# Sinkhorn-sorted attention with a StarReLU layer behind it: the first microseconds reordered, the last outputs cut finer

## The chip, the cores and the metric

The kernel runs on one core of one Trainium2 chip. A core has five engines that run their own instruction queues in order: TensorE (matrix products, with weight loads listed as PEld), VectorE (DVE), ScalarE (ACT), GpSimd (POOL) and SyncE (SP). TensorE writes to PSUM; VectorE and ScalarE copy from PSUM to SBUF. DMAs are issued from SyncE's and GpSimd's queues. The metric is the device time of one execution in microseconds (us). Three runs of the kernel before took 223.43, 222.94 and 223.51 us; the median is 223.43.

## The reference

Four batches, eight heads, 768 tokens, head size 64. Each head has an 8 by 8 sorting matrix, made nearly doubly stochastic by five rounds of Sinkhorn; it mixes blocks of 96 keys and of 96 values, and each block of queries attends to its sorted block alone. The outputs of all heads side by side go through a layer of width 2048.

```python
P = sort_net
for _ in range(5):
    P = P - np.max(P, axis=-1, keepdims=True)
    P = np.exp(P)
    P = P / (np.sum(P, axis=-1, keepdims=True) + 1e-09)
    P = P / (np.sum(P, axis=-2, keepdims=True) + 1e-09)
k_sorted = np.einsum('bhij,bhjcd->bhicd', P, k_b)      # v_sorted likewise
scores = scale * np.matmul(q_b, k_sb.transpose(0, 1, 2, 4, 3))
attn = softmax(scores)                                  # per block, + 1e-09 in the sum
x = np.matmul(attn, v_sb)                               # heads side by side: 3072 x 512
r = np.maximum(x @ w_in, 0.0)
out = (s * (r * r) + b) @ w_out                         # 3072 x 512, float32
```

## The kernel before, in words

The order of the work is written out by hand: each engine runs its instructions in the order in which the program issues them, and buffers come from rotating pools. In PSUM, pool `psa` has three tiles of two banks (keys, values, scores, `pv`, hidden sums) and pool `psb` two tiles of one bank (transposes, half key pieces, scores in banks, outputs). A tile of a pool can be written only when the tile that last had its buffer has been read.

**Loads.** SyncE loads the sorting matrices (L77) and the values of batch 0 in four quarters of 12 columns, `v0f` (L81). GpSimd issues all other loads: half of the queries (`qh`), the keys in three parts (`rawk`), then, after small constants, `w_in` in slices (`wi`, L142), the other half of the queries, `w_out`, and data of batch 1. GpSimd's issues hold on for older loads: at most eight are under way.

**Front, batch 0, first half.** TensorE begins with matmuls on zeros (`warm`, L132): 16 of 256 columns, 108 of 96, 6 of 512. Meanwhile VectorE and ScalarE run Sinkhorn on `sn`, 32 heads on 32 partitions (L231 to L253); between its exponentials ScalarE casts the quarters of `v0f` into `VP[0]` (`permute`, L196). Then `spread_first` copies batch 0's rows to 128 partitions by a matmul (`pe`, L259), and `build_pd` (L275 to L284) makes of them a block-diagonal matrix `pd` with which a matmul sorts, divided by a sum `cs` for the rounding left by the last, unfinished column step.

After that come, in this order: query transposes `q_banks` (L218); key tiles of 16 columns, two of a full `psa` tile (`k_piece`, L294) and one in two banks (`k_banks`, L320); the first of four value tiles (`v_piece`, L330); the rows of all four batches spread into a corner of a score tile and copied to `later` (`spread_all`, L259 and L271); scores of the first two head pairs (`s_banks` L399, `s_piece` L381) with their exponentials; the other value tiles; scores of the other pairs; per head pair the product with the values, divided by its sum (`p_piece`, L423 to L429), and its transpose to `xt` (`t_piece`, L440); and the first two double columns of the hidden layer, by head pairs (`part`, L474). `evac` copies a PSUM tile with the engine named by its letter, "D" for VectorE (L206) and "A" for ScalarE (L204). A number after the head pair in `p_piece` and `part` asks for so many fill matmuls on zeros before the real ones (L417, L469).

**Dense part.** Then come, for each half batch t of 384 tokens, `ffn1` (hidden layer, ReLU on ScalarE, square on VectorE) and `ffn2` (second product, `ops`, L498), with the attention work of the following halves put in slots between them. For batches 2 and 3 the values are sorted as rows, and `v_back` sends them through a DRAM buffer `vd` (L355) to the layout `VS` (L359); the query transposes by DMA (L457) stand behind it in SyncE's queue.

**End.** The last half batch has three row groups of 128 tokens. The last of them is computed in two halves of 256 output columns (L511). `store` scales by `s` and adds the bias on VectorE (L519) and issues the DMA (L522).

## Time and profile before

| What | Value |
|---|---|
| profiled execution | 223.59 us |
| its span | 221.8 us |
| median of three runs | 223.43 us (222.94 to 223.51) |
| TensorE busy | 214.8 us, 97% of the span |
| VectorE, ScalarE, GpSimd busy | 123.3, 106.1, 70.6 us |
| first `tqb` transposes of the dense part start | 26.43 us |
| last matmul of the program starts | 218.13 us |
| last DMA is issued, lands | 218.95, 220.66 us |

The profile is of one execution. Times are counted from the span's start. In rows of the timeline the columns are start, duration (of a merged run of like instructions: from the first start to the last end), engine, line, operation, output and inputs, shapes, the number of instructions, and in brackets how long the engine was idle before and what ended that. In rows of the chain they are start, length, engine and line. In rows by line, what stands behind the bar is busy time, mean length of one instruction in ns, and idle time before. Matmuls are pipelined: one starts before the one ahead has ended, so the distance of their starts tells the occupancy, not their length.

### The profile page before, as it was taken

The numbers are of one execution on the slowest core, as the hardware profiler recorded it, in microseconds if no ns is written. First come the engines' busy times: TensorE is split into PE (matmuls) and PEld (weight loads), VectorE is DVE, ScalarE is ACT, GpSimd is POOL, SyncE is SP. The second block draws the span as 40 slices with busy tenths as digits, with TensorE's granted clock in tenths as the row PEclk, the third lists the DMA queues.
The fourth block names the chain that finished last, engine by engine and source line by source line (L and its number), as shares of the span: only waits on it lengthen the run. The fifth ranks groups of instructions, "written<-read, shape, count | busy, mean of one in ns | idle before, by whom it ended". The sixth has DMA issues, their size and how long they took to land.

```text
span 221.8 us, 5257 instructions
## 1 busy us (share of the span) xinstructions
PE 214.8 (97%) x2212; PEld 129.6 (58%) x2231; DVE 123.3 (56%) x251; ACT 106.1 (48%) x144; POOL 70.6 (32%) x127
## 2 busy tenths in 40 slices
PE   7999999999999999999999999999999999999993
PEld 5977766555655555666446555655446556654453
DVE  6767457549754767546616677548417744442121
ACT  4677687656144344664622535665424355650000
POOL 7659791669914004930032008800000000000000
PEclk9999999999999999999999999999999999999999
DMA  6999999999999632999999546999911440001212
GB/s 154 280 165 126 125 162 207 204 177 117 116 182 165 183 96 46 138 236 127 91 252 171 138 121 91 236 147 92 221 69 50 121 120 0 0 3 47 95 47 95
DMA packets 66935, 28.92 MB, mean 130 GB/s; under 512 B 51808, under 2 KB 62816, under 8 KB 66912
## 3 DMA queue, kind: packets, MB, share of 16 engines
q0 software_dynamic: 31168, 12.85, 49.6%
q1 hardware_dynamic: 35744, 15.74, 34.3%
q8 instruction: 17, 0.28, 0.6%
q14 instruction: 6, 0.05, 0.1%
HBM read 28.85 MB, written 7.86 MB: 165 GB/s over the span
## 4 chain that ended last, share of the span: by engine, by line
PE 95%; DVE 2%; issue 1%; ACT 0%
PE hps L474 38%; PE ops L498 36%; PE z L132 5%; PE pv L423 4%; PE sc L381 3%; PE ops L511 2%; PE tv L330 2%; PE tp L294 1%; PE tpp L304 1%; PE tvr L349 1%; DVE vs L206 1%; PE tr L440 1%; PE scb L399 1%; PE sc L259 0%; PE pv L417 0%
## 5 line engine op out<-in xcount | busy, mean ns | idle before, releaser
L474 PE MATMUL hps<-xt,wi 128*128 128x384 bf16 x512 | 87.9, 326 | 0.0
L498 PE MATMUL ops<-wo,gt 128*128 128x512 bf16 x350 | 82.4, 379 | 1.5 <-issue 0.8
L486 ACT ACTIVATE rt<-hps 128x768 bf16<-128x768 f32 x64 | 51.8, 811 | 39.5 <-PE hps L474 38.8
L474 PEld LDWEIGHTS <-wi 128*128 128x128 bf16 x512 | 49.0, 98 | 32.6 <-issue 0.4
L487 DVE TENSOR_TENSOR gt<-rt 128x768 bf16<-128x768 bf16 x64 | 35.6, 558 | 41.2 <-ACT rt L486 41.0
L498 PEld LDWEIGHTS <-gt 128*128 128x128 bf16 x368 | 34.0, 98 | 37.2
L519 DVE SCALAR_TENSOR_TENSOR ot<-ops,s_bc,bias 128x512 f32<-128x512 f32 (+1 forms) x25 | 18.2, 729 | 37.9 <-PE ops L498 34.4
L389 ACT ACTIVATE at<-sc 112x768 bf16<-112x768 f32 x24 | 18.1, 808 | 31.8 <-PE sc L381 31.8
L429 DVE TENSOR_TENSOR x<-pv,rec 96x512 bf16<-96x512 f32 x32 | 22.0, 687 | 1.1
L116 POOL DMA_DIRECT2D qtok<-in_q_dram x24 | 18.6, 810 | 0.7 <-DMA rawk<-in_k_dram 0.6
L423 PEld LDWEIGHTS <-at 112*128 112x128 bf16 (+1 forms) x256 | 12.9, 101 | 6.7 <-ACT at L389 1.0
L142 POOL DMA_DIRECT2D wi<-in_moe_w_in_dram x24 | 13.0, 583 | 6.0 <-DMA qh<-in_q_dram 3.1
L423 PE MATMUL pv<-vs,at 112*128 112x66 bf16 (+1 forms) x256 | 13.9, 195 | 0.1
L93 POOL DMA_DIRECT2D rawk<-in_k_dram x21 | 11.2, 551 | 4.3 <-DMA rawv<-in_v_dram 2.0
L132 PE MATMUL z<-zeros 128*64 128x96 bf16 (+2 forms) x129 | 10.8, 257 | 1.3 <-DVE zeros L120 1.2
L93 POOL DMA_DIRECT2D rawv<-in_v_dram x18 | 9.7, 555 | 5.5 <-DMA wo<-in_moe_w_out_dram 4.7
L204 ACT CAST ks<-tpp 64x512 bf16<-64x512 f32 x12 | 8.7, 725 | 4.4 <-DVE ks L206 4.1
L132 PEld LDWEIGHTS <-zeros 128*64 128x64 bf16 (+1 forms) x130 | 8.5, 128 | 3.0 <-DVE zeros L120 1.2
L90 POOL COPY rawk<-xt 128x1 bf16<-128x1 bf16 x2 | 0.4, 190 | 31.1 <-DMA xt<-x 31.1
L428 DVE RECIPROCAL rec<-pv 96x8 f32<-96x8 f32 x32 | 6.4, 200 | 6.4 <-PE pv L423 6.4
L206 DVE CAST ks<-tpp 64x512 bf16<-64x512 f32 x12 | 8.7, 728 | 0.2
L351 DVE CAST rawv<-tvr 128x512 bf16<-128x512 f32 x12 | 8.2, 683 | 0.0
(93 smaller groups left out, 141.6 us busy)
## 6 DMA issues: line engine op xcount, KB each, us to landing
out_dram<-ot SPq DMA_DIRECT2D x23, 256.0 KB, 2.5
rawv<-in_v_dram POOLq DMA_DIRECT2D x18, 128.0 KB, 5.1
rawk<-in_k_dram POOLq DMA_DIRECT2D x18, 128.0 KB, 4.5
qtok<-in_q_dram POOLq DMA_DIRECT2D x24, 96.0 KB, 6.7
wo<-in_moe_w_out_dram POOLq DMA_DIRECT2D x4, 512.0 KB, 10.4
v0f<-in_v_dram SPq DMA_DIRECT2D x4, 384.0 KB, 7.1
vd<-rawv SPq DMA_DIRECT2D x2, 768.0 KB, 6.8
vs<-vd SPq DMA_DIRECT2D x8, 192.0 KB, 7.4
```

The source lines that it names most:

```text
L93: nc.gpsimd.dma_start(out=ti[:, c:c + n, :].rearrange("p c d -> p (c d)"), in_=raw["qkv".index(t)][b][:, c * D:(c + n) * D])
L116: nc.gpsimd.dma_start(out=ti[:, n + h], in_=qv[:, n + h])
L132: nc.tensor.matmul(out=z[0:m, 0:w], lhsT=zeros[:, 0:m], rhs=zeros[:, 0:w], start=True, stop=True)
L142: nc.gpsimd.dma_start(out=wi[:, al, f0:f1], in_=wiv[:, al, f0:f1])
L389: nc.scalar.activation(out=at, in_=sc[0:KR, :, 0:TG], func=AF.Exp, scale=scale)
L423: nc.tensor.matmul(out=pv[0:m, e, n * VW:(n + 1) * VW], lhsT=atf[:, c0:c0 + m], rhs=VS[b % 2][:, e * NG + g0 + n, :], start=True, stop=True)
L429: nc.vector.tensor_tensor(out=x[:, :, hp * 128:(hp + 1) * 128].rearrange("p n (e d) -> p e n d", e=2), in0=pvv[:, :, :, 0:D], in1=rec.unsq ...
L474: nc.tensor.matmul(out=H1[t, i][:, f, 0:TG], lhsT=wi[:, hp, fc:fc + 128], rhs=XT[t][:, :, hp, :], start=(hp == 0), stop=(hp == NHP - 1))
L486: nc.scalar.activation(out=rt, in_=h, func=AF.Relu)
L487: nc.vector.tensor_tensor(out=gt[:, 2 * i:2 * i + 2, :], in0=rt, in1=rt, op=ALU.mult)
L498: nc.tensor.matmul(out=ops, lhsT=gt[:, f, m * 128:(m + 1) * 128], rhs=wo[:, f, :], start=(f == 0), stop=(f == NF - 1))
L519: nc.vector.scalar_tensor_tensor(out=ot[:, ns], in0=ops, scalar=s_bc, in1=BIAS[0][:, ns], op0=ALU.mult, op1=ALU.add)
```

## The change

In the front: 1e-9 stands as a ninth row in the Sinkhorn tile, so the first column sum takes it in and the separate add goes. `build_pd` gets its sum `cs` from the product itself (`accum_out`) in place of a second reduce. The warm-up has 132 matmuls of 72 columns in place of 108 of 96. The third quarter of `v0f` is cast by GpSimd, behind four `wi` issues. The first value tile is issued ahead of the key tiles, and ScalarE empties it; the spread of the three later batches gets a tile of its own between key tiles and half key pieces; value tiles 3 and 4 are emptied half by ScalarE and half by VectorE; scores 2 and 3 use whole tiles and stand between the p pieces; fill matmuls are gone; `part` takes two head pairs at once. `v_back` sends the two halves of the partitions as two DMAs and reads them back in that order. At the end, the last but one row group is stored in two halves, and the last row group is computed and stored in 256, 128 and 128 columns.

```diff
-    sn = const.tile([BH, NB, NB], FP)
+    sne = const.tile([BH, NB + 1, NB], FP)
+    sn = sne[:, 0:NB, :]
...
     for c in range(4):
         for a in range(NHP):
             load_wi(c * W8, (c + 1) * W8, slice(a, a + 1))
+        if c == 0:
+            permute(nc.gpsimd, 0, v0f, slice(2 * CV, 3 * CV))
...
-    eps = const.tile([BH, NB], FP)
-    nc.vector.memset(eps, 1e-9)
+    nc.vector.memset(sne[:, NB:NB + 1, :], 1e-9)
...
-    warm(108, 96, 64)
+    warm(132, 72, 64)
...
-        for c in {1: (0,), 3: (1,), 4: (2, 3)}.get(it, ()):
+        for c in {1: (0,), 3: (1,), 4: (3,)}.get(it, ()):
...
-        nc.vector.tensor_reduce(out=rstat, in_=sn.rearrange("p i j -> p j i"),
+        nc.vector.tensor_reduce(out=rstat, in_=(sn if it else sne).rearrange("p i j -> p j i"),
                                 axis=AX.X, op=ALU.add)
-        if it == 0:
-            nc.vector.tensor_tensor(out=rstat, in0=rstat, in1=eps, op=ALU.add)
...
-    def spread_all(ps):
-        for b in range(B):
-            o = TG + b // 2 * NB * NB
-            spread_rows(b, ps[:, b % 2, o:o + NB * NB])
-        nc.scalar.copy(out=later.rearrange("p u w n -> p u (w n)"), in_=ps[:, :, TG:512])
+    def spread_later():
+        pe = psa.tile([128, B - 1, NB * NB], FP, tag="a", name="pel")
+        for b in range(1, B):
+            spread_rows(b, pe[:, b - 1, :])
+        return lambda: nc.scalar.copy(out=later, in_=pe)
...
-        nc.vector.tensor_tensor(out=tmp, in0=rows.rearrange("p (i j) -> p i j", j=NB),
-                                in1=spread(jsel, [[0, NB], list(jsel.ap[1])]), op=ALU.mult)
+        cs = rtp.tile([128, 1], FP, tag="cs", name="cs")
+        nc.vector.scalar_tensor_tensor(
+            out=tmp, in0=rows.rearrange("p (i j) -> p i j", j=NB), scalar=1.0,
+            in1=spread(jsel, [[0, NB], list(jsel.ap[1])]), op0=ALU.mult, op1=ALU.mult, accum_out=cs)
         pt = rtp.tile([128, NB], FP, tag="pt", name="pt")
         nc.vector.tensor_reduce(out=pt, in_=tmp, axis=AX.X, op=ALU.add)
-        cs = rtp.tile([128, 1], FP, tag="cs", name="cs")
-        nc.vector.tensor_reduce(out=cs, in_=pt, axis=AX.X, op=ALU.add)
...
-        nc.sync.dma_start(out=vd.rearrange("e z g c d -> (e z g) (c d)"),
-                          in_=RAW["v", b].rearrange("p c d -> p (c d)"))
-        for z in range(2):
-            for e in range(2):
+        for e in range(2):
+            nc.sync.dma_start(out=vd[e].rearrange("z g c d -> (z g) (c d)"),
+                              in_=RAW["v", b][e * 64:(e + 1) * 64].rearrange("p c d -> p (c d)"))
+        for e in range(2):
+            for z in range(2):
...
-                    if f == NF - 1:
+                    if f == NF - 1 and last and m == TG // 128 - 2:
+                        for n0 in range(0, d_model, d_model // 2):
+                            ns = slice(n0, n0 + d_model // 2)
+                            store(t, m, ops[:, ns], ns)
+                    elif f == NF - 1:
                         store(t, m, ops)
...
-            for n0 in range(0, d_model, d_model // 2):
-                ns = slice(n0, n0 + d_model // 2)
-                ops = psb.tile([128, d_model // 2], FP, tag="b", name="ops")
+            for n0, w in ((0, 256), (256, 128), (384, 128)):
+                ns = slice(n0, n0 + w)
+                ops = psb.tile([128, w], FP, tag="b", name="ops")
...
     q_banks(0, 0, "DA")
+    v_piece(0, 0, "A")
     k_piece(0, 0, "D")
     k_piece(0, CK, "A")
+    copy_later = spread_later()
     k_banks(0, 2 * CK, "DA")
-    v_piece(0, 0, "D")
-    sc1 = psa.tile([128, 2, 512], FP, tag="a", name="sc")
-    spread_all(sc1)
+    copy_later()
     s_banks(0, 0, 0)
-    s_piece(0, 0, 1, sc1)
+    s_piece(0, 0, 1)
     v_piece(0, CK, "D")
-    v2 = v_piece(0, 2 * CK, "D", 1)
+    v2 = v_piece(0, 2 * CK, "A", 1)
+    v2("D")
     v3 = v_piece(0, 3 * CK, "A", 1)
-    v2("D")
-    s_banks(0, 0, 2)
-    p_piece(0, 0, 0, 3)
-    v3("A")
-    p_piece(0, 0, 1, 2)
-    s_banks(0, 0, 3)
-    p_piece(0, 0, 2, 2)
+    v3("D")
+    s_piece(0, 0, 2)
+    p_piece(0, 0, 0)
+    s_piece(0, 0, 3)
+    p_piece(0, 0, 1)
+    p_piece(0, 0, 2)
     t_piece(0, 0, 0, "A")
-    p_piece(0, 0, 3, 3)
+    p_piece(0, 0, 3)
     t_piece(0, 0, 1, "A")
-    part(0, 0, (0,), 3)
-    part(0, 1, (0,), 2)
+    part(0, 0, (0, 1))
     t_piece(0, 0, 2, "A")
-    part(0, 0, (1,))
-    part(0, 1, (1,))
-    t_piece(0, 0, 3, "A")
+    part(0, 1, (0, 1))
+    t_piece(0, 0, 3, "D")
```

More of the change, by code (lines that the diff above doesn't have):

```diff
@@ L147, in fill_vs, with permute @@
         nc.gpsimd.memset(VS[i][32:C2, :, D:VW], 1.0)
+    def permute(eng, b, src, cs=slice(0, C2), ds=slice(0, D)):
+        o = VP[b % 2][:, ds, cs]
+        i = src[:, cs, ds].rearrange("p c d -> p d c")
+        if eng is nc.scalar:
+            eng.copy(out=o, in_=i)
+        else:
+            eng.tensor_copy(out=o, in_=i)
     load_qh(0, 0)
@@ L190 @@
     idv = ident.rearrange("p (a e j z) -> p a e j z", a=NHP, e=2, j=NB)
-    def permute(eng, b, src, cs=slice(0, C2), ds=slice(0, D)):
-        o = VP[b % 2][:, ds, cs]
-        i = src[:, cs, ds].rearrange("p c d -> p d c")
-        if eng is nc.scalar:
-            eng.copy(out=o, in_=i)
-        else:
-            eng.tensor_copy(out=o, in_=i)
     QT = {}
@@ L255 @@
     PD = {}
-    later = const.tile([128, 2, B // 2, NB * NB], FP)
+    later = const.tile([128, B - 1, NB * NB], FP)
     def spread_rows(b, o):
@@ L593, in TD, with PDB @@
     def TD(b, h): return lambda: t_dma(b, h)
-    def PDB(b): return lambda: build_pd(b, later[:, b % 2, b // 2, :])
+    def PDB(b): return lambda: build_pd(b, later[:, b - 1, :])
     def QD(b): return lambda: q_dma(b)
```

## The prediction, made before the changed kernel was run

> **What bounds the kernel now.** I read the page first (engine shares, chain by engine), then the chain in order of time, the timeline of the first 27 us and of the last 6, the groups by line for prices, the stage windows and the DMA issues.

> ```profile
> PE 214.8 (97%) x2212; PEld 129.6 (58%) x2231; DVE 123.3 (56%) x251; ACT 106.1 (48%) x144; POOL 70.6 (32%) x127
> PE 95%; DVE 2%; issue 1%; ACT 0%
> ```

> TensorE bounds the kernel: from 26.5 us on the chain is TensorE work without a wait over 0.16 us, so what the change does to the front arrives at the end one for one, and only three places can move the time: when TensorE reaches the first `tqb` of the dense part, what is done after its last matmul, and its clock. The chain through the front, from the view in order of time:

> ```profile
> 12.03 0.37 PE pe L259 x2
> 13.34 0.36 DVE pd L284
> 13.74 1.20 PE tp L294 x64
> 15.96 1.04 PE sc L259 x8
> 18.46 2.43 DVE vs L206 x3
> 20.94 0.38 PE pv L417 x2
> 26.50 0.88 PE tqb L218 x48
> ```

> The path runs: Sinkhorn and warm-up, the diagonal weights `pd` (ready at 13.69), key matmuls, the row spread, VectorE's copies of the values, then the p/t/hidden pieces. The last line is the front's finishing post: its transposes start at 26.43 in the timeline. Beside it, off the chain today, stands this row of the timeline:

> ```profile
> 12.18 1.54 ACT L196 CAST vp<-v0f 128x768 bf16<-128x768 f32 x1 [0.39 <-DMA v0f<-in_v_dram]
> ```

> The fourth quarter of the first values lands at 12.15 and is cast by 13.72. Its reader, the first value tile, starts at 15.26, so it has 1.5 us of slack. The tail, from the timeline and from the DMA issues after 210 us:

> ```profile
> 214.95 0.75 DVE L519 SCALAR_TENSOR_TENSOR ot<-ops,s_bc,bias 128x512 f32<-128x512 f32 x1 [2.70 <-PE ops L498]
> 216.69 0.48 DVE L519 SCALAR_TENSOR_TENSOR ot<-ops,s_bc,bias 128x256 f32<-128x256 f32 x1 [1.00 <-PE ops L511]
> 218.44 0.48 DVE L519 SCALAR_TENSOR_TENSOR ot<-ops,s_bc,bias 128x256 f32<-128x256 f32 x1 [1.26 <-PE ops L511]
> out_dram<-ot SPq DMA_DIRECT2D x2, 256.0 KB, 2.0
> out_dram<-ot SPq DMA_DIRECT2D x2, 128.0 KB, 1.7
> ```

> KB are of one DMA, the last number its time from issue to landing. The last store is computed by 218.93, issued at 218.95, lands at 220.66, and SyncE's closing waits fill the rest of the 221.8 us span.

> **Part 1: Sinkhorn, warm-up, `pd`.** The add of 1e-9 leaves (0.16 us, with its hand-over 0.2); the column sum over nine rows instead of eight grows by under 0.03 (0.21 to 0.25 for 64 elements); the memset keeps its place. Sinkhorn ends 0.17 to 0.2 earlier, at about 10.9. The warm-up, not Sinkhorn, releases `pe` today: its last matmul starts at 11.65, Sinkhorn ended at 11.08. New warm-up: single matmuls of 96 columns come every 80 ns until about 7.18 and every 42.5 ns after. In proportion 72 columns take 60 ns and 32 to 35. The slow stretch of 2.45 us holds 41 of them; the other 91 take 2.9 to 3.2, against 3.27 today. `pe` starts 0.1 to 0.35 earlier. In `build_pd` one reduce (0.16 and 0.03) goes, and the reciprocal no longer waits for `pt`. The product with an accumulated sum has no row; its nearest are the plain product (0.23) and the scalar-tensor-tensor on 128 elements (0.35), and I take 0.3, between 0.22 and 0.5. `pd` is ready at 13.1 to 13.4, 0.3 to 0.6 earlier. Worth on the path: nothing, because of part 2.

> **Part 2: the third quarter on GpSimd, values ahead of keys.** The cast stands behind four `wi` issues (done at 8.67) and waits for the landing at 10.02. Its nearest row is GpSimd's strided copy of the later values:

> ```profile
> L198 POOL COPY vp<-rawv 128x384 bf16<-128x384 bf16 x4 | 3.2, 853 | 0.0
> ```

> Twice the elements: 1.7 us. The 512-element float copy (0.61) gives 0.9 as the low end; twice the row is 3.4. It ends at 11.8, between 10.9 and 13.4, always before ScalarE's fourth quarter. Behind it on GpSimd wait `wi` issues 5 to 8. Today they go at 10.10, 11.33, 12.56 and 14.66, each held by the landing of an older load. Three of them go up to 2 us later; the fourth still waits for the key landing of 14.38, so everything behind keeps its time. Their data lands at 16.1 behind older transfers and is first read after 23.9. Cost 0; with that cover gone, up to 2 us.

> ScalarE gains nothing by giving the quarter away: it sat idle from 11.78 to 12.15 and still casts the last quarter until 13.72. The first value tile now leads TensorE's queue and needs all four quarters: it starts at 13.75, where the first key tile starts today (13.74). The 0.3 to 0.6 of part 1 ends in this wait. Queued behind the waiting tile are all key pieces, which only needed `pd`.

> **Part 3: the order from there**, with these prices: a 32-matmul piece occupies TensorE 0.51 and its result is there 0.70 after its start; a half piece 0.25 and 0.45; four row spreads 1.15, so three 0.91; copies of 1024 columns 1.22 on VectorE and 1.01 on ScalarE, of 512 0.68 and 0.59; exponentials 0.49 a bank and 0.82 a pair; a hand-over 0.03 to 0.04; a queued follower starts 0.1 before its predecessor's end.
> - Values 13.75, keys 14.26 and 14.76. ScalarE empties the value tile 14.49 to 15.50. The three-row spread takes the value tile's buffer, since three tiles are out: 15.54 to 16.45.
> - The key half pieces stand behind the spread: 16.45 and 16.70; ScalarE's copy of the second ends at 17.77. The first scores start at 17.81, today 16.92. Today the value tile and the spread cover those copies; now nothing does: +0.9.
> - ScalarE has the spread's copy, scores 0 (to 19.07) and scores 1 (to 19.78). The fourth value tile takes scores 1's buffer: 19.82, there at 20.52. ScalarE's half of it ends at 21.15. The first p piece starts at 21.19; today 20.43, so +0.76.
> - Then reciprocal and product per p piece on VectorE (0.86 each), the second `xt` copy ends at 24.29, and TensorE has to run eight hidden matmuls, two transpose pieces and six more hidden matmuls: 0.65+0.17+0.65+0.17+0.98 brings the `tqb` to 26.95.

> The same bookkeeping applied to today's order gives 26.25 where the trace has 26.43. So the front loses 0.52 against the trace and 0.70 like against like; I take **+0.6**. The removed fill matmuls (0.11 and 0.055 each, 15 in all) lie in waits, and are worth nothing in this sum. The lower bound of this stage is VectorE's chain: 3.44 us from first reciprocal to last product, then transpose and hidden work without TensorE's queue in between: 26.3, a gain of 0.15.

> **Part 4: `v_back`.** SyncE issues one more DMA per call (0.33), twice. The reload of the first half can start before the second half lands (one transfer took 7.4, 90.8 to 98.2), and the query transposes queued behind land at 112.2 for scores at 114.45. Cost 0; were this slack of 2.2 us gone, at most the 0.7 of issue. The shorter `build_pd` later is off the path.

> **Part 5: the last outputs.** Columns 256, 128, 128: 16 matmuls at 0.109 and 32 at about 0.056 (the filler of 128 columns comes every 57 ns) take 3.53 to 3.59 against 3.49: +0.06. The last store works on 128 columns: 0.75 and 0.48 put a column at 1.04 ns, so 0.35: -0.13. The last DMA has 64 KB: 2.0 for 256 and 1.7 for 128 give 1.55: -0.15, between 0 and -0.3. SyncE closes with nine waits 0.06 apart over eight completion flags taken in turn; today the last DMA's flag is the fifth, and four waits follow it. Four more DMAs (two in `v_back`, two stores) move it to the ninth: -0.24. The split store of the tile before ends by 215.9, before its buffer is wanted at 216.5: 0. Sum **-0.45**, between -0.2 and -0.6.

> **Sum.** +0.6 - 0.45 = +0.15. The profiled execution took 223.59 (span 221.8 and 1.8 around it): 223.74. The median shown is 0.16 lower, 223.43, which gives 223.58. I take 223.7.

> **Rivals.**
> 1. *The clock falls.* The removed fills kept TensorE busy between 19.8 and 24.1. In these windows (busy time with count in brackets: TensorE, weight loads, VectorE, ScalarE, GpSimd, then clock, DMA share, GB/s) the same work runs at two speeds:

> ```profile
> 1.20:7.20 6.00, 6.00 (x48) 4.72 (x49) 4.77 (x22) 3.22 (x6) 5.61 (x14) 1.00 0.90 225
> 7.20:10.50 3.30, 3.30 (x80) 3.30 (x78) 2.35 (x12) 2.06 (x4) 1.87 (x4) 1.00 1.12 277
> 20.40:23.50 3.10, 2.99 (x58) 2.66 (x59) 2.99 (x8) 2.45 (x6) 3.10 (x7) 1.00 1.09 141
> ```

> TensorE was slow for its first 6 us although busy, and the granted-clock column does not show it. After the change TensorE works about half the time from 20.6 to 24.0, in gaps of at most 0.7 us. If that sends it back to the slow rate, dense work loses half of the slow stretch: up to 3.0 us for a stretch like the first, 1.5 for half of it: 225.2 to 226.8. It decides from a slow stretch of 1.1 us. Against it: a gap of 0.47 at 13.3 left the speed alone.

> [...]

> 2. *The value landing sets the pace and comes later.* Today the cast has 1.5 us of cover; afterwards each 0.1 us of a later landing is 0.1 us of time. Quarters land 3.5, 2.0 and 2.1 us apart against the key and query loads. One microsecond later: 224.7; it decides from 0.5. Against it: the transfers issued before 10 us are the same.

> 3. *Faster.* The front comes out even or at its lower bound (26.3 to 26.4), by an earlier landing or by p pieces that interleave better than my bookkeeping: -0.15 to 0, with the tail's -0.45 to -0.6: 222.8 to 223.1. For it: VectorE gives 1.2 us of copies away to ScalarE, fills leave. Against it: ScalarE then has 5.9 us of work between 14.49 and the first p piece, so that cannot start before 20.4 even without a wait.

> **Chances.** My forecast 0.5 (223.2 to 224.2), clock 0.12, late landing 0.18, faster 0.2. A measurement of this kernel can tell about 0.3%, 0.67 us: below 222.76 is faster, above 224.10 slower. From the cases: faster takes 0.16 (most of case 3, which reaches the bound only with both ends good), slower 0.36 (cases 1 and 2 and the forecast's upper edge), within 0.48. The range of 8 in 10 runs from case 3's low end to past case 2 and the lower clock case: 222.6 to 225.4.

> **What would show it.** Right: `pd` at 13.1 to 13.4 with an idle TensorE until the fourth quarter's cast ends near 13.7; first scores near 17.8; first p piece near 21.2; the dense part's first `tqb` near 27.0; GpSimd's cast over by 12; last DMA issued about 0.1 earlier with a shorter landing and one closing wait. Wrong: matmuls of 384 columns further apart than 163 ns after 20 us (rival 1), the fourth quarter cast after 14.2 (rival 2), the first p piece before 20.6 (rival 3), or a wait of TensorE in the dense part.

## The result, and the profile after

The changed kernel takes 224.07 us (median of 22 runs, 223.54 to 228.34); the kernel before, in as many runs beside it, 223.41 (222.94 to 225.46). The ratio is 1.0042, with a 95% interval of 1.0024 to 1.0059: slower by 0.2 to 0.6%. One thing must be known to read these numbers: in 10 of the 22 executions TensorE's granted clock was below 0.995 on average (median 225.94; the ratio leaves out the two slowest of them), in the other 12, called undisturbed below, it was 0.998 or more (median 223.68), so the typical undisturbed loss is 0.27 us and the rest goes with the clock.

The profiled execution (223.69 us, span 221.9) is one at full clock. Its page:

```profile
PE 212.4 (96%) x2235; PEld 127.4 (57%) x2254; DVE 122.9 (55%) x252; ACT 105.2 (47%) x141; POOL 72.1 (32%) x128
PE 89%; DVE 5%; ACT 3%; issue 1%; DMA 1%
```

Still TensorE's kernel, but the chain now runs through VectorE and ScalarE for 8% of the span: the front. The lines of the chain in order of time that answer to those of before:

```profile
9.05 1.37 DVE sne L247
...
12.32 0.41 PE pe L259 x2
...
13.35 0.36 DVE pd L284
13.75 0.71 PE tv L330 x32
14.48 1.03 ACT vs L206
15.56 0.88 PE pel L259 x6
...
17.10 0.59 ACT ks L206
17.74 0.39 PE scb L400 x8
...
20.47 0.60 ACT vs L206
...
27.09 0.87 PE tqb L220 x48
```

The chain begins with Sinkhorn, not with the warm-up, and holds a product of 32x64 numbers that took 1.37 us. Then it runs as forecast: value tile at 13.75, its copy, the spread, the half key pieces' copy, first scores at 17.74 (16.92 before), fourth value tile's copy, and the dense part's first `tqb` at 27.02 (26.43). The timeline shows why the product is long:

```profile
8.82 1.50 POOL L156 CAST vp<-v0f 128x768 bf16<-128x768 f32 x1
8.83 0.19 DVE L246 RECIPROCAL rrec<-rstat 32x8 f32<-32x8 f32 x1
9.05 1.36 DVE L247 TENSOR_TENSOR sne<-sne,rrec 32x64 f32<-32x64 f32 x1
10.45 0.26 DVE L250 TENSOR_REDUCE rstat<-sne 32x8 f32<-32x64 f32 x1
...
11.37 1.48 ACT L154 CAST vp<-v0f 128x768 bf16<-128x768 f32 x1
...
11.96 0.21 DVE L247 TENSOR_TENSOR sne<-sne,rrec 32x64 f32<-32x64 f32 x1
```

The same product takes 0.21 us at 11.96. At 9.05 GpSimd was in the middle of its cast (8.82 to 10.33); the product ended at 10.41, 0.08 after it. The reciprocal at 8.83, with one input, ran beside the cast in 0.19 us, as long as the one at 11.73. So the product, which reads `sne` and `rrec`, waited here for the rest of the cast and was 1.15 us longer; why it waits, no row shows. The profiles of e4 and e11 below repeat it: 1.29 and 1.32 us, ending 0.08 after the cast.

The tail, from the timeline:

```profile
217.28 0.48 DVE L524 SCALAR_TENSOR_TENSOR ot<-ops,s_bc,bias 128x256 f32<-128x256 f32 x1 [0.87 <-PE ops L516]
218.18 0.35 DVE L524 SCALAR_TENSOR_TENSOR ot<-ops,s_bc,bias 128x128 f32<-128x128 f32 x1 [0.41 <-PE ops L516]
219.07 0.35 DVE L524 SCALAR_TENSOR_TENSOR ot<-ops,s_bc,bias 128x128 f32<-128x128 f32 x1 [0.54 <-PE ops L516]
```

The last DMA is issued at 219.45 and lands at 221.00, 1.55 later (1.71 before), and a single closing wait follows. From the first `tqb` to the span's end it is 194.90 us against 195.39: the tail and the dense part give back 0.49 of the 0.59 that the front loses. Net in the profiles: +0.1. The stretch repeats: of the other profiles with the new end (e1, e2, e4, e5, e8 to e12) all but e11's have 194.9, and those with the old one (e3, e6, e7) 195.4, whatever the front does.

### The profile page after: what moved, and what is told of

The parts are those of the page before. It is cut to its first block, busy times and chain, and to the rows that moved or that the text cites. A ratio compares the mean times of both kernels' runs of the same rounds, so it can differ in the third digit from the quotient of the medians.

```text
span 221.9 us, 5311 instructions
## 1 busy us (share of the span) xinstructions
PE 212.4 (96%) x2235; PEld 127.4 (57%) x2254; DVE 122.9 (55%) x252; ACT 105.2 (47%) x141; POOL 72.1 (32%) x128
## 4 chain that ended last, share of the span: by engine, by line
PE 89%; DVE 5%; ACT 3%; issue 1%; DMA 1%
PE hps L475 38%; PE ops L499 36%; PE pv L424 4%; PE sc L382 2%; PE tv L330 2%; PE ops L516 2%; PE tpp L304 1%; PE tvr L349 1%; DVE sne L247 1%; DMA sne<-in_sort_net_dram 1%; PE tp L294 1%; ACT vs L206 1%; PE tr L441 1%; PE scb L400 1%; ACT sne L240 1%
## 5 line engine op out<-in xcount | busy, mean ns | idle before, releaser
L524 DVE SCALAR_TENSOR_TENSOR ot<-ops,s_bc,bias 128x512 f32<-128x512 f32 (+2 forms) x27 | 18.6, 691 | 39.0 <-PE ops L499 35.0
L206 ACT CAST ks<-tpp 64x512 bf16<-64x512 f32 x12 | 8.7, 725 | 4.3 <-DVE ks L208 4.1
L133 PE MATMUL z<-zeros 128*64 128x72 bf16 (+2 forms) x153 | 9.5, 230 | 1.3 <-DVE zeros L121 1.2
L133 PEld LDWEIGHTS <-zeros 128*64 128x64 bf16 (+1 forms) x154 | 7.3, 118 | 3.0 <-DVE zeros L121 1.2
## 6 DMA issues: line engine op xcount, KB each, us to landing
out_dram<-ot SPq DMA_DIRECT2D x22, 256.0 KB, 2.6
rawv<-in_v_dram POOLq DMA_DIRECT2D x18, 128.0 KB, 5.4
rawk<-in_k_dram POOLq DMA_DIRECT2D x18, 128.0 KB, 4.6
```

Source lines behind the costliest of these rows:

```text
L133: nc.tensor.matmul(out=z[0:m, 0:w], lhsT=zeros[:, 0:m], rhs=zeros[:, 0:w], start=True, stop=True)
L524: nc.vector.scalar_tensor_tensor(out=ot[:, ns], in0=ops, scalar=s_bc, in1=BIAS[0][:, ns], op0=ALU.mult, op1=ALU.add)
```

## The experiments

The theories. **A**: GpSimd's cast holds a VectorE product until it ends. **B**, of the prediction: the cast is free, the fourth quarter's arrival sets the start. **Clock 1**: the thin stretch after 20 us lets the clock fall; **clock 2**: the gap ahead of `pe` does. **D**, formed later: TensorE's instruction stream is not loaded in time. (**A2**, a variant of A in e5: the hold lasts until GpSimd has no more such work.) Each run's ratio is to the kernel before, run beside it on the same chip.

### e1: the third quarter back on ScalarE

```diff
-        if c == 0:
-            permute(nc.gpsimd, 0, v0f, slice(2 * CV, 3 * CV))
...
-        for c in {1: (0,), 3: (1,), 4: (3,)}.get(it, ()):
+        for c in {1: (0,), 3: (1,), 4: (2, 3)}.get(it, ()):
```

> The changed kernel with the third quarter cast by ScalarE again; all else as changed. Theory A (GpSimd's cast holds a VectorE product with two SBUF inputs until the cast ends: 1.36 us against 0.21 in the changed kernel's profile): no Sinkhorn product over 0.25 us, Sinkhorn ends near 11.0, pd ready at 12.5 to 12.6 in place of 13.70; the first value tile then starts as soon as ScalarE has cast both last quarters (13.1 to 13.8), and the time falls by 0 to 0.6 against the changed kernel. Theory B (as predicted: the landing and cast of the fourth quarter set the start and GpSimd's cast is free): products at 0.21 in both, first value tile at 13.7, the time unchanged within 0.2.

223.64 us, ratio 1.0012 (0.9989 to 1.0034). VectorE's timeline, and then TensorE's:

```profile
10.81 0.21 DVE L245 TENSOR_TENSOR sne<-sne,rrec 32x64 f32<-32x64 f32 x1
...
12.20 0.35 DVE L282 SCALAR_TENSOR_TENSOR pd<-bm,rc,pt 128x128 bf16<-128x128 f32 x1
```

```profile
13.20 0.70 PE L328 MATMUL tv<-pd,vp 128*64 128x64 bf16 x32 [0.74 <-ACT vp L154]
```

All products at 0.21, Sinkhorn ends at 11.02, `pd` is ready at 12.55: A holds, and 1.15 us of the changed kernel's `pd` is GpSimd's. The value tile then waits for ScalarE's two casts (10.22 to 13.15): B's wait exists as well, but it stood behind A's in the changed kernel. First scores at 17.19, 0.55 earlier than in the changed kernel, of which 0.32 is left at the first `tqb` (26.70); where the other 0.23 goes is told at e9. In time e1 lies between the kernel before and the changed kernel: 3 of its 12 executions were below 0.995, the other nine have a median of 223.50.

### e5 and e6: the cast in four parts; the cast alone

```diff
-            permute(nc.gpsimd, 0, v0f, slice(2 * CV, 3 * CV))
+            for i in range(4):
+                permute(nc.gpsimd, 0, v0f, slice(2 * CV + 3 * i, 2 * CV + 3 * i + 3))
```

> The changed kernel with GpSimd's cast cut in four instructions of 3 columns (0.4 to 0.5 us each). Theory A, a held product waits for the end of the one GpSimd instruction that it met: no Sinkhorn product longer than about 0.6 us, one to three of them lengthened, Sinkhorn ends at 11.3 to 11.9 in place of 12.17. Rival A2, it waits until GpSimd has no more such work: one product of 1.3 us or more as with the single cast. Theory B: all products 0.21. Time 0 to 0.4 below the changed kernel.

In the timeline of e5's profiled execution (222.94 us, full clock):

```profile
8.62 1.66 POOL L156 CAST vp<-v0f 128x192 bf16<-128x192 f32 x4
8.82 0.19 DVE L247 RECIPROCAL rrec<-rstat 32x8 f32<-32x8 f32 x1
9.05 0.46 DVE L248 TENSOR_TENSOR sne<-sne,rrec 32x64 f32<-32x64 f32 x1
9.55 0.26 DVE L251 TENSOR_REDUCE rstat<-sne 32x8 f32<-32x64 f32 x1
9.84 0.19 DVE L253 RECIPROCAL rrec<-rstat 32x8 f32<-32x8 f32 x1
10.06 0.23 DVE L254 TENSOR_TENSOR sne<-sne,rrec 32x64 f32<-32x64 f32 x1
```

The product that meets a part (8.98 to 9.50) ends at 9.51, after that part and not after all four. A holds and A2 falls: the hold (0.46 us in place of 0.21) lasted to the end of one GpSimd instruction. `pd` is ready at 12.83, the dense part starts at 26.27. Still the median is 224.34 (1.0071, 1.0040 to 1.0101), because the clock was below 0.995 in 6 of 10 executions; the other four have a median of 223.64.

e6 puts only the cast (and ScalarE's shorter list) into the kernel before.

> The kernel before with only the third quarter cast by GpSimd. Theory A: one Sinkhorn product of 1.1 to 1.5 us, Sinkhorn ends near 12.3 in place of 11.08, pd near 14.1 in place of 13.69, dense part 0.3 to 0.9 later: 223.8 to 224.4, and in some executions a granted clock below 1.0 through the gap ahead of pe. Theory B: nothing moves, 223.5.

224.18 us, ratio 1.0032 (1.0013 to 1.0051). The cast met another product:

```profile
9.47 1.52 POOL L155 CAST vp<-v0f 128x768 bf16<-128x768 f32 x1 [0.81 <-DMA v0f<-in_v_dram]
9.73 0.19 DVE L254 RECIPROCAL rrec<-rstat 32x8 f32<-32x8 f32 x1
9.96 1.11 DVE L255 TENSOR_TENSOR sn<-sn,rrec 32x64 f32<-32x64 f32 x1
```

It is 1.11 us long and ends 0.08 after the cast. Alone, and without the rest of the change, the cast costs 0.67 us of the median (0.21 at the first `tqb` of the profiled execution, 223.79, one of the two fastest of ten). A stands; which product is hit depends on when the quarter lands (8.77 in the changed kernel, 9.41 here).

### e2: the end alone

e2 puts the changes of `ffn2` and `v_back`, and nothing else, into the kernel before.

> The kernel before with only the last outputs in parts and v_back in two DMAs. Prediction's part 5: the last DMA issued 0.1 earlier, landing 0.15 sooner, one closing wait in place of five (0.24): 0.45 to 0.5 less than before, 222.9. Rival: the tail is bound by something else (TensorE's narrower matmuls, the bias product) and the time stays within 0.15 of before.

223.13 us against 223.53, ratio 0.9977 (0.9959 to 0.9994): -0.40. From the first `tqb` to the end it is 194.9 us, as in the changed kernel. This part of the change is a gain. The outputs and `v_back` were not run apart.

### e3: the order alone

e3 puts the new list of front pieces and `spread_later` into the kernel before; ScalarE casts all quarters.

> The kernel before with only the new order of the front's pieces (values ahead of keys, spread ahead of the half key pieces, new engines for the copies, no fills); Sinkhorn, warm-up, casts and tail as before. Prediction's part 3: first scores near 17.8 in place of 16.92, first p piece near 21.2 in place of 20.43, dense part 0.5 to 0.7 later: 223.9 to 224.1. Rival (the order is neutral, and the loss in the changed kernel's front comes from Sinkhorn's held product): first scores by 17.2, the time within 0.2 of before.

223.90 us, ratio 1.0011 (0.9995 to 1.0026). TensorE's timeline:

```profile
13.31 0.70 PE L330 MATMUL tv<-pd,vp 128*64 128x64 bf16 x32 [0.73 <-ACT vp L196]
...
15.93 0.69 PE L320 MATMUL tkb<-pd,rawk 128*64 128x64 bf16 x32
17.30 0.34 PE L399 MATMUL scb<-qt,ks 64*128 64x96 bf16 x8 [0.68 <-ACT ks L204]
```

From the first tile to the first scores it takes 3.99 us, in the changed kernel 3.99, in the kernel before 3.18: the order costs 0.8 there, 0.9 forecast. From the first tile to the first `tqb` it is 13.27 here and in the changed kernel, against 12.69 before: 0.58, the +0.6 of the forecast. So the changed kernel's front, whose first tile starts where it did before (13.75 against 13.74), loses its 0.59 by the order; the held product used up the 0.55 by which e1's first tile is earlier. The time alone would not show it, as the interval of the ratio holds 1. What softens the loss here is the start: the fourth quarter landed at 10.21, not at 12.15 as in the one profile of before, so the value tile starts at 13.31. `pd` was ready at 12.99, because the warm-up ended early: full speed began at 4.5 us here and at 7.17 there. Both moved from execution to execution without any edit.

### e4 and e11: what lets the clock fall

e4 puts the 15 fill matmuls back into the changed kernel; e11 lengthens its warm-up.

```diff
-    warm(6)
+    warm(14)
```

> The changed kernel with the fill matmuls of the p and hidden pieces put back (3, 2, 2, 3 and 3, 2). Clock theory 1 (the thin stretch from 20.6 to 24 lets the clock fall in some executions: 10 of 22 of the changed kernel had a mean granted clock below 1.0): all executions at 1.00, typical time 223.6 to 223.8 as in the undisturbed ones. Clock theory 2 (the 1.5 us gap ahead of pe, which the held product makes, lets it fall): as many executions below 1.0 as without the fills.

> The changed kernel with 14 in place of 6 matmuls of 512 columns at the end of the warm-up, 1.7 us more, so that TensorE is busy while GpSimd's cast holds Sinkhorn. Clock theory 2 (the gap of 1.5 us ahead of pe, not the thin stretch later, lets the clock fall): no execution, or one in ten, below 0.995, the median 223.6 to 223.8. Clock theory 1 (the thin stretch from 20.6): as many below 0.995 as in the changed kernel (10 of 22), median 224.0 or more.

e4: 225.10 us (1.0063, 1.0039 to 1.0087), one of seven executions below 0.995, the profiled one. e11: 225.96 us (1.0088, 1.0057 to 1.0120), four of six below 0.995. Stage windows of e4 and then of e11 (columns as in the prediction):

```profile
10.88:14.30 3.42, 1.88 (x87) 1.83 (x89) 2.20 (x10) 2.34 (x3) 1.47 (x4) 1.00 1.21 198
14.30:24.54 10.24, 9.44 (x242) 8.60 (x236) 4.53 (x5) 6.39 (x11) 9.52 (x19) 0.50 1.01 119
24.54:28.00 3.46, 3.06 (x54) 2.52 (x54) 3.26 (x8) 1.77 (x3) 2.21 (x5) 1.00 1.04 127
```

```profile
15.70:19.11 3.41, 2.63 (x85) 2.17 (x84) 1.51 (x2) 2.43 (x6) 3.41 (x7) 1.00 0.82 96
19.11:22.53 3.42, 3.18 (x96) 2.92 (x91) 2.51 (x3) 2.86 (x5) 3.42 (x7) 0.50 1.06 125
22.53:25.94 3.41, 2.33 (x42) 1.65 (x42) 2.78 (x8) 1.84 (x4) 2.99 (x6) 1.00 1.00 119
25.94:29.35 3.41, 3.39 (x17) 1.92 (x17) 1.00 (x3) 0.48 (x1) 1.86 (x4) 0.50 1.08 147
```

The clock's changes lie whole multiples of 3.41 us apart: 3.41 or 3.42 in e11 (from 19.11 on), 10.24 in e4, three of them, and full clock is recorded for 218.45 us, 64 of them, in the changed kernel's profile and for 215.04, 63, in that of before. The phase of this grid differs between the profiles: full clock begins at 5.15 and 7.17 in the last two. In e4 it falls after the window with the gap ahead of `pe` (1.97 us without a matmul) and stays at half for three windows; in e11, which has no such gap, it falls twice, each time after a thin window of the front. So each clock theory is half right: after both spots it fell here, and each cure leaves the other open.

How thin a window must be, I worked out from the matmul records of the thirteen profiles that record the clock's changes (e5's does not): columns at the dense part's rate (512 in 216 ns, halved where the clock is), weighted with the size of the weights as a share of the largest, 128x128, float32 counted four times (the row spread's matmuls of 64 columns start 112 ns apart in the profile of before, where 64 columns at that rate take 27). The weighting with the size is my choice; no run tests it. In these profiles windows of 0.39 and more never let it fall (the changed kernel's five thinnest are 0.40 to 0.49); windows of 0.10 (e9), 0.26 (e4), 0.33 and 0.38 (both e11) did; one of 0.36 (e10) and one of 0.38 (e1) did not. The kernel before has no window below 0.46, and none of the 83 executions of it beside the twelve experiments was below 0.995. The limit near 0.38 is read off these windows and was not tested by itself. If the grid is slid over the changed kernel's profile (windows between 7 and 35 us), about three quarters of its phases have a window below 0.37 (the thinnest 0.18), and over that of the kernel before no phase has one below 0.44; that this is why the clock falls in some executions of the changed kernel and not in others is an inference, since none of those that fell was profiled. It is also not the whole account: e2, with the front of before, and e12, whose thinnest windows in any phase are 0.48 and 0.43, had one execution of twelve at 0.992 each, and e4, with a window below 0.37 in about 7 of 10 phases, fell once in seven.

The fills themselves are not free in the new order: the six executions of e4 at full clock have a median of 225.0, 1.5 above the kernel before beside them, where the changed kernel's undisturbed ones lie 0.27 above. Which wait they make was not seen, since the profiled execution fell to half clock.

### e7 and e8: starting early without GpSimd

e7 is the kernel before with the ninth row, the accumulated sum and the new warm-up. e8 adds the new end and moves one line:

```diff
+    v_piece(0, 0, "D")
     k_banks(0, 2 * CK, "DA")
-    v_piece(0, 0, "D")
```

> The kernel before with only the ninth row, the accumulated sum and the new warm-up; the old order, ScalarE's casts, the old tail. pd at 12.5 to 12.6, first key tile at 12.6 in place of 13.74. The half key pieces then wait for the third key load (landing 14.4): first scores 0.3 earlier, 223.2. Rival (the front is bound by the copies, not by its start): within 0.1 of before. Rival (bound by its start): 1.1 less, 222.4.

> A version meant to beat both: the kernel before with the ninth row, accumulated sum, new warm-up, tail and v_back of the change, the casts on ScalarE, the old order except that the first value tile stands between the full key tiles and the half key pieces, which wait for the third key load. pd 12.5, first scores at 16.2 to 16.5 in place of 16.92, first p piece near 19.8 in place of 20.43, dense part 0.6 to 0.8 earlier, tail 0.45 less: 222.1 to 222.5. If only the tail counts: 223.0.

e7: 224.27 us (1.0037, 1.0025 to 1.0049). e8: 223.69 us (1.0009, 0.9997 to 1.0020). Both miss. The first key tile does start at 12.65 and 12.59, and the first p piece's reciprocal comes at 20.59 and 20.52 (20.89 before), but the dense part starts at 26.67 and 27.02. e8's timeline, TensorE:

```profile
20.54 0.38 PE L416 MATMUL pv<-zeros 128*128 128x240 bf16 x2
20.76 0.32 PE L422 MATMUL pv<-vs,at 112*128 112x66 bf16 x5
21.90 0.28 PE L422 MATMUL pv<-vs,at 112*128 112x66 bf16 x3 [0.82 <-issue]
```

Eight matmuls of one p piece, whose inputs are all there since the first, stop after five for 0.82 us, with no releaser. e7 stops at the same place for 0.37. In each, the stop is longer than what the front was ahead by at the reciprocal (0.37 in e8, 0.30 in e7). e7's profiled execution, 223.82, is its fastest of five; what made the others slower was not seen.

### e9 and e10: fewer TensorE instructions; other copy engines

```diff
-    warm(132, 72, 64)
-    warm(6)
+    warm(27)
```

> The version of e8 with a warm-up of 16 matmuls of 256 columns and 27 of 512 in place of 154 small ones: the same length, 222 TensorE instructions fewer. In e7 and e8 TensorE stood still for 0.37 and 0.82 us in the middle of a p piece, at its 961st instruction in both, with no semaphore to wait for. Theory D (the next block of TensorE's instruction stream is not there yet when the front starts early; blocks are 256 instructions, 16 KB a fetch): the wait is gone from that place, the dense part starts at 25.7 to 26.2 in place of 27.0, and the time is 222.3 to 222.8. Rival (something of the p pieces themselves): the wait stays in the same piece, 223.5 to 223.7.

> e9 with the copies of the queries, the first key tile, the second key tile, the first value tile and half of the third dealt D D, A, D, A, A in place of D A, D, A, D, D. By the prediction's bookkeeping first scores at 16.2 in place of 16.6 and the dense part 0.3 earlier than in e9: 222.0 to 222.5. Rival (the front is then bound by the loads): equal to e9.

e9: 225.09 us (1.0080, 1.0054 to 1.0106), five of six executions below 0.995; e10: 225.15 us (1.0069, 1.0056 to 1.0082), three of five. Both miss, and tell the most. The wait left the p piece and came back earlier and longer; e9's TensorE, and the queue that the page calls instruction:

```profile
14.74 0.43 PE L256 MATMUL sc<-sne,emat 32*128 32x64 f32 x2
17.29 0.88 PE L256 MATMUL sc<-sne,emat 32*128 32x64 f32 x6 [2.12 <-issue]
```

```profile
q8 instruction: 17, 0.28, 0.5%
```

Counted from 0 over TensorE's records (matmuls, weight loads and those of its sequencer), TensorE stood before these, and the last fetch on that queue before the wait's end began at:

| kernel | record | waited, us | fetch began | wait ended |
|---|---|---|---|---|
| e9 | 450 | 2.12 | 15.01 | 17.29 |
| e10 | 450 | 1.87 | 15.17 | 17.61 |
| e10 | 705 | 0.38 | 19.56 | 21.98 |
| e7 | 961 | 0.37 | 19.11 | 21.55 |
| e8 | 961 | 0.82 | 19.56 | 21.90 |
| e11 | 963 | 0.47 | 20.64 | 23.40 |

The places lie 255 to 258 apart whatever stands there in the program, e9's 17 fetches (0.28 MB together, so 16 KB each) answer to its 4,346 records (256 each; other kernels have 17 or 18 for 4,345 to 4,563), and each wait but e11's ends 2.3 to 2.4 us after a fetch began (e11: 2.8). The kernels that did not stop fit as well: in none of the fourteen profiles do the records 450, 706 and 962 start earlier than 2.28 us after the first, second and third fetch began. The kernel before passes them at 2.6, 2.6 and 2.8, the changed kernel at 3.6, 2.4 and 2.6, so neither front had much room. e1 was at the edge: at record 961, 2.36 after the fetch, two matmuls of a p piece start 0.25 apart in place of 0.03, which answers to the 0.23 that it lost after its first scores. That the wait is for the next block of instructions is an inference that these numbers support well, though no run changed the fetch alone. In the front a fetch begins every 3.5 to 6.5 us, behind it mostly every 5 to 25. By this reading, taking instructions out of the warm-up moved the block's edge deeper into the busy front, so e9 and e10 met it sooner, at record 450 (their first fetch began at 15.01 and 15.17, in the other kernels at 9.9 to 11.8; why so late was not seen). e10's dealing of copies could not show itself behind this wait.

### e12: the gain that is left

> The kernel before with the ninth row, the accumulated sum, the new tail and v_back, but with the old warm-up of 108 matmuls, old order, casts on ScalarE: e7 and e2 together without the new warm-up. Theory D (TensorE's instruction blocks: 48 instructions fewer than in e7 put the block's edge elsewhere): no wait of TensorE without a releaser over 0.2 us in the p pieces, pd at 12.6 to 13.4, dense part 0.1 to 0.4 earlier than before, time 222.7 to 223.0, below the tail alone (223.1). Rival: the wait comes at another piece and the time is that of e8, 223.5 to 223.7. Clock: every window of the front stays as full as in the kernel before, so no execution below 0.995.

223.01 us against 223.46, ratio 0.9980 (0.9965 to 0.9995). No wait without a releaser over 0.2 us: by D, the old warm-up puts the block's edge where it holds nothing up. But it is no better than the tail alone (e2, 0.9977). `pe` starts at 11.71, released by the warm-up, the fourth quarter landed only at 12.66 in this execution, so that ScalarE's copy of the queries, behind its cast, ended at 14.91, and first scores come at 16.88 (16.92 before). One of twelve executions was at 0.992. Both e2 and e12 beat both kernels; nothing in the front did by itself.

## Why the prediction was right or wrong, point by point

The forecast of 223.7 us, no measurable change, with 224.07 measured, stands within its range, though the interval of the ratio, 1.0024 to 1.0059, shows a small loss and not none. The undisturbed executions' 223.68 hits it by some luck: one wait took the place of another at the same time.

- *Part 1, Sinkhorn and `pd`.* Right in its terms: Sinkhorn, from its first reduction to its last product, takes 8.52 to 8.59 us where no product is held (e1, e7 to e10, e12), against 8.69 to 8.71 before (also e2, e3), 0.10 to 0.19 less with 0.17 to 0.2 forecast; from `pe` to `pd` it takes 1.38 us in place of 1.73, and the product with the accumulated sum measured 0.23 and 0.08 for the read-out, against the 0.3 taken.
- *Part 2, GpSimd's cast at cost 0.* This step failed. Its length was right (1.50 against 1.7) and the delayed `wi` loads cost nothing, but beside it on VectorE ran Sinkhorn's products, which the step did not look at. It held `pd` back by 1.15 us, so `pd` came at 13.70, not at 13.1 to 13.4.
- *Part 2, the value tile at 13.75 by the fourth quarter's landing.* Right number, wrong reason: the quarter landed at 10.47 and was cast by 12.84; `pd`, ready at 13.70, released the tile. Of two waits the forecast named the one that came second here; e1 and e3 show it first, at 13.20 and 13.31. The 12.15 was one execution's draw: 10.06 to 12.66 were seen.
- *Part 3, the order.* Right: scores at 17.74 (17.81 forecast), first p piece at 21.12 (21.19), `tqb` at 27.02 (26.95). The mechanism, key copies and ScalarE's list uncovered, is what the chain shows, and its size, 0.58 against +0.6, is what e3 shows. "Worth nothing" for the fills was wrong: in this order putting them back costs about 1.2 us (e4, undisturbed, each against the kernel before beside it), and the stretch without them is one of the two thin ones.
- *Part 4* cost nothing, as said. *Part 5*: -0.49 in the profiles, -0.40 in e2's medians, -0.45 forecast. Its terms come out one by one, counted from the first `tqb`: the last DMA is issued 0.09 earlier (0.07 forecast), it takes 0.16 less (0.15), and the closing waits 0.24 less (0.24).
- *Rival 1, the clock*, given 0.12, came in 10 of 22 executions and makes 0.4 of the median's 0.66. The evidence against it, one gap of 0.47 us, was too little: the window around that gap was still 0.48 full. *Rival 2*, a later landing, did not occur; *rival 3* fell, and e7 to e10 point to a second reason beside ScalarE's load: TensorE stood there for 0.37 to 2.12 us with no releaser, by D for its next instructions.

## What to carry to other kernels

Before work goes to an idle GpSimd, look at what VectorE does in those microseconds: here a two-input product that met the cast waited for its end, and in a chain of dependent 0.2 us steps that was 1.15 us. Fill matmuls and warm-up went here with two things that a sum of durations does not show: how full each 3.41 us window was (0.46 and more in the kernel before, and no fall in 83 executions; 0.40 and more in the changed kernel's profile, and 10 of 22 executions below 0.995), and where TensorE met the edges of its 256-record blocks (waits of 0.37 to 2.12 us in five experiments). So an order that looks a little slower can be the safer one. Cutting the last outputs finer, with `v_back` in halves, was the one part that paid by itself.
